# SBUF layout of a fused attention, SoLU and ReLU² kernel: stationary and moving operands of layer 2 on opposite sides

## The chip, the cores and the metric

The kernel runs on one core of a Trainium2 chip. The metric is the device time of one execution in microseconds (us), lower is better. Three runs of the kernel before gave 858.24, 858.86 and 859.9 us, a median of 858.86 us. The profiled execution is a further run, of 858.75 us.

## The reference

```python
scores = q @ k.T / 8 + cum[:, None] - cum[None, :]     # cum = cumsum(log(clip(f))), causal mask
attn   = softmax(scores) @ v                           # 4 batches, 8 heads, 576 tokens, head size 64
x      = attn as [2304 tokens, 512]
h      = x @ w_in                                      # layer 1, w_in [512, 1024]
solu   = h * softmax(h)
x      = layernorm(solu) * g_ln @ w_out                # w_out [1024, 512]
out    = maximum(x @ w2_in, 0) ** 2 @ w2_out           # layer 2, w2_in [512, 2048], w2_out [2048, 512]
```

All of it is float32. The kernel multiplies in fp32r: each operand is split into a high part and the rest, `h` and `l`, and a product is made of three matmuls (high by low, low by high, high by high).

## The kernel before

One program holds attention, layer 1 and layer 2. Each piece of work is added to a planner (`Plan.add`) with its reads, its writes, a priority and a guessed duration for every engine that may do it; `lay` then writes one fixed order for each engine from the guesses. Priorities are planned times: layer 2's weights get `TEND + W20 + p * W2P`, its steps `TEND + P2 + 5200` apart, where `TEND` is the planned end of attention. All DMAs are issued on SyncE's queue in the planned order.

**Layer 2.** The 2,304 tokens are 9 blocks of 256 (`TB`), and the 2,048 hidden features are 8 pairs of 128-wide chunks (`KP`, counted by `p`). `step(blk, p)` has:

- 24 up matmuls (L1175): the stationary operand is a 128x128 piece of the pair's `u` weights (`u0h`, `u0l`, `u1h`, `u1l`), the moving one 256 columns of the block's x tiles (`x2t`, named `vn` in the trace).
- ReLU and square on ScalarE (L1193, L1197), four sums and differences on VectorE (L1204), and the split into `GA`/`GS` by `halves`: the high part by a cast on ScalarE (L341), the rest by a subtraction (L1059) on GpSimd or VectorE, as the planner finds.
- 21 down matmuls (L1229 to L1231): seven products by a Strassen-like scheme, 9 matmuls for group A and 12 for group S; stationary is `GA` or `GS` (named `q` in the trace), moving are 256 columns of the pair's `a`, `b`, `s`, `t` weights.

So a block has 8 x 45 = 360 matmuls of 256 columns and layer 2 has 3,240. TensorE runs the ups of one step, then the downs of the step before it.

`weights2(p)` brings the weights of pair `p` once, between layer 1 and block 0: four loads of 256 KB from `w2d` into raw tiles (`raws`, in turn by `RING`), five splits of 512 and one of 256 columns (`halves`), and four differences of 256 (`diff`, L1096), on GpSimd or VectorE.

**Where tiles lie.** SBUF is handed out in the order of the calls of `new`, so the address of a tile is the sum of the sizes before it. Layer 2 has no room of its own: `carve` reuses the tiles of attention and layer 1 once they are free, and the lists `large` (512 columns), `small` (256) and `upper` (512, taken by the `u` weights of pairs 5 to 7) are filled by `more` and emptied by `place`. In KiB of a partition, counted from the first tile: `maskb` 0, `wih` 1.3, `wil`, `woh`, `wol` to 65, `k1`, `k2` to 109, `qn`, `adj`, `pt`, `x`, `xh`, `xl`, `e`, `free`, `xw` to 157.3, small vectors and `q3`, then `ws` from 159.8, `xc`, `ident` 165.8, `q1` 166.3, `q2` 174.3, `vn` 182.3, `kn` 194.3, `ln` 198.3 to 222.3.

By this the up matmuls have their weights low (`free`, `k1`, `k2`, `pt`, `wih`, `wil`) for pairs 0 to 4 and high (`ln`) for pairs 5 to 7, and their x tiles high (`vn`). The down matmuls have `q1`/`q2` high as stationary and most weights low; the `a` weights of pairs 4 to 7 lie in `ws`, `xc` and `kn`, high.

**Double buffering.** `x2slot` has six x tiles: the first half of a block's features (g = 0) has two sets, the second half one, so that the second half of the next block is loaded after the last ups of this one. At a change of block the ups are done in two lots of 12.

Layer 1's last stage is `out1` (L773 to L775: stationary `woh`/`wol`, moving `ln`). PSUM has three free banks `pp`, of which one is held by `seven` through a block, and two banks `hp` that are layer 1's until block 1.

```python
        for a in "hl":
            W[nm + a] = (small if n == 256 else upper if nm[0] == "u" and p >= KP - 3 else large).pop(0)
            claim(W[nm + a], [("w2", p, nm + a)], prio)
...
    def x2slot(blk, a, g):
        return (0, 1, 4, 5)[2 * (blk % 2) + a] if g == 0 else 2 + a
```

Of the kernel before, what the change touches and what calls it, by code (L numbers as in the profile page):

```python
# [8 lines left out]
F32 = mybir.dt.float32  # L9
F32R = mybir.dt.float32r  # L10
# [3 lines left out]
ALU = mybir.AluOpType  # L14
# [226 lines left out]
def tile_kernel(ctx: ExitStack, tc: tile.TileContext, q, k, v, f, w_in, w_out, g_ln, w2_in, w2_out, out):  # L241
    nc = tc.nc
# [48 lines left out]
    K1 = [new(f"k1{j}", [HH, KW], F32R) for j in range(2)]  # L291
    K2 = [new(f"k2{j}", [HH, KW], F32R) for j in range(2)]
    QN = new("qn", [DM])
    ADJ = [new(f"adj{i}", [AW]) for i in range(NADJ)]
    PT = [new(f"pt{i}", [5 * P]) for i in range(NPT)]
    X = new("x", [NP, P])
# [4 lines left out]
    new("xw", [256])  # L301
    ST = [new(f"st{i}", [2]) for i in range(NST)]
# [3 lines left out]
    new("q3", [512])  # L306
    new("ws", [768])
    new("xc", [768])


    ident = new("ident", [P])
    Q1 = [[new(f"q1{i}{j}", [HH, P], F32R) for j in range(2)] for i in range(2)]
    Q2 = [[new(f"q2{i}{j}", [HH, P], F32R) for j in range(2)] for i in range(2)]
    VN = [new(f"vn{i}", [DM]) for i in range(NV)]
    KN = [new(f"kn{i}", [DM]) for i in range(2)]
# [444 lines left out]
    def out1(blk, ccs, prio, dp):  # L760
# [3 lines left out]
        for cc in ccs:  # L764
            w = slice(cc * P, cc * P + P)
            sk = key()
            for g in range(4):
                def fn(g=g, sk=sk, w=w):
                    px = at(sk)[:, 0 : 2 * P].rearrange("p (r x) -> p r x", x=P)
                    for fc in (2 * g, 2 * g + 1):  # L770
                        hi = LN["h"][:, fc, ring[0] : ring[1] + 1 : step, :]
                        lo = LN["l"][:, fc, ring[0] : ring[1] + 1 : step, :]
                        nc.tensor.matmul(px, lhsT=woh[:, fc, w], rhs=lo, start=(fc == 0), stop=False)  # L773
                        nc.tensor.matmul(px, lhsT=wol[:, fc, w], rhs=hi, start=False, stop=False)  # L774
                        nc.tensor.matmul(px, lhsT=woh[:, fc, w], rhs=hi, start=False, stop=(fc == KF - 1))  # L775

                rk = [(a, r, g // 2) for a in ("lnh", "lnl") for r in ring]
                rk += [("wo", fc, cc // 2, a) for fc in (2 * g, 2 * g + 1) for a in "hl"]
                pl.add(dict(pe=714), fn, prio, rk, [sk], take=sk if g == 0 else None, uses=[sk] if g else [])
                prio += dp / 4  # L780
# [175 lines left out]
    held["maskb"] = ["mask"]  # L956
    held["free"] = [("fr", i, z) for i in range(5) for z in "lh"] + [("fw", i) for i in range(5)]
# [21 lines left out]
    def rk2(ri):  # L979
        return [("2r", ri, z) for z in range(2)]  # L980
# [9 lines left out]
    for j in range(2):  # L990
        more(f"k1{j}", 5, 1)
        more(f"k2{j}", 5, 1)
# [6 lines left out]
    more("xl0", 1)  # L999
    more("e", 2)  # L1000
    for a in ("woh", "wol"):
        more(a, 8)
    for a in ("ln0", "ln1"):
        more(a, 6, 0, upper)
# [3 lines left out]
    for i in range(2):  # L1008
        small.extend(carve(f"kn{i}", [256, 256], old=rk2(i)))
    more("xc", 0, 3)  # L1010
    GS = [carve(f"q1{i}{j}", [512])[0] for i in range(2) for j in range(2)]
    GA = [carve(f"q2{i}{j}", [384])[0] for i in range(2) for j in range(2)]
    x2t = [carve(f"vn{i}", [512])[0] for i in range(4)]
    raws = [carve(a, [512], F32)[0] for a in ("kn0", "kn1", "adj1", "adj2", "vn4", "vn5", "pt4", "x")]

    x2t += [carve(f"vn{i + 4}", [512], old=rk2(i + 4))[0] for i in range(2)]
# [7 lines left out]
    RING = [n % 8 for n in range(4 * (KP - 2))] + [2 + n % 6 for n in range(8)]  # L1024
# [90 lines left out]
    def x2slot(blk, a, g):  # L1115
        return (0, 1, 4, 5)[2 * (blk % 2) + a] if g == 0 else 2 + a
# [38 lines left out]
    def step(blk, p, prio):  # L1155
        g = (blk * KP + p) % 2
        uid[0] += 1
        pool = "hp" if blk and g else "pp"
# [5 lines left out]
        if (blk, p) == (1, 1):  # L1164
            pl.add(dict(dve=0), lambda: None, prio - 5000, [], ["h", "hp"])
        W = W2[p]
        for y, c in ((0, 0), (0, 1), (1, 0), (1, 1)):
# [15 lines left out]
            pl.add(dict(pe=6 * 116), up, prio, rk, [ck], take=None if y + c else ck, uses=[ck] if y + c else [])  # L1183
# [258 lines left out]
W20, W2P, P2 = 30000, 5000, 30000  # L1442
# [53 lines left out]
```

## Time and profile before

| | |
|---|---|
| median of three runs | 858.86 us |
| profiled execution | 858.75 us |
| its span in the trace | 857.0 us |
| around the span | 1.75 us |
| TensorE (PE) busy | 812.9 us, 95% |
| VectorE (DVE) busy | 569.3 us, 66% |
| ScalarE (ACT) busy | 548.7 us, 64% |
| GpSimd (POOL) busy | 396.2 us, 46% |
| DMA | 87.5 MB, 32.7% of 16 engines' span |

PE is matmuls, PEld weight loads, which overlap them; L1175 is line 1175 of the kernel. Matmuls are pipelined: one row of 256 columns shows 0.28 us, but the next one starts 0.11 to 0.12 us later. The distance from start to start is what a matmul costs, and a row that merges n of them lasts n - 1 distances and one 0.28. Times on a timeline are us from the start of the span. A wait is put down to what ended it.

### The profile page before, as it was taken

Reading aid. Unit: us, or ns where it says so; the run is one execution under the profiler, and the core shown is the slowest. Engines: PE = TensorE matmul, PEld = TensorE weight load, DVE = VectorE, ACT = ScalarE, POOL = GpSimd, SP = SyncE. Lnnn points to the kernel's source line nnn. Section 1 sums busy time; section 2 is a strip of 40 time slices with the busy share of each in tenths; the row PEclk is TensorE's granted clock in tenths of the full one; section 3 lists DMA queues with packets and bytes.
Section 4 is the critical chain, followed back from the end, with each engine's and each line's share of the span. In section 5 each row is a group of like instructions: output and inputs, shape, how many; then the busy total and the mean of one; then the engine's idle time right before and its main releaser. Section 6 shows DMA issues by size and latency. Waiting matters only on the chain.

```text
span 857.0 us, 18172 instructions
## 1 busy us (share of the span) xinstructions
PE 812.9 (95%) x6584; PEld 745.0 (87%) x6584; DVE 569.3 (66%) x1371; ACT 548.7 (64%) x1343; POOL 396.2 (46%) x480
## 2 busy tenths in 40 slices
PE   3778999999999999999999989999999999999997
PEld 2556787888888887889899989999999999999996
DVE  7898777878799868855557785454545454554544
ACT  6889989888887878766755644444444444444442
POOL 7547777665676546631397763131312121222221
PEclk9988999999999999999999989999999999999999
DMA  6644336656575565510263330101010101010100
GB/s 206 189 136 134 98 107 196 206 160 195 180 220 161 179 178 164 159 51 26 63 194 114 97 114 26 50 26 50 25 50 26 51 25 50 26 50 26 28 24 25
DMA packets 69338, 87.52 MB, mean 102 GB/s; under 512 B 8480, under 2 KB 46880, under 8 KB 69248
## 3 DMA queue, kind: packets, MB, share of 16 engines
q1 hardware_dynamic: 69248, 86.37, 32.7%
q8 instruction: 51, 0.84, 0.4%
q14 instruction: 39, 0.32, 0.1%
HBM read 63.58 MB, written 22.69 MB: 101 GB/s over the span
## 4 chain that ended last, share of the span: by engine, by line
PE 75%; DVE 10%; ACT 9%; issue 2%; DMA 2%; POOL 1%; SPq 1%; ACTq 0%; DVEq 0%; POOLq 0%
PE pp L1175 12%; PE hp L1175 11%; PE pp L586 5%; PE z L532 4%; PE xo L606 4%; PE z L1230 4%; PE z L1229 4%; PE z L1231 4%; PE hp L832 3%; PE hp L834 3%; PE hp L833 3%; ACT adj L567 3%; PE pp L773 3%; PE pp L774 3%; PE pp L775 3%
## 5 line engine op out<-in xcount | busy, mean ns | idle before, releaser
L1059 POOL TENSOR_TENSOR q<-q,q 128x384 fp32r<-128x384 f32 x72 | 76.6, 1064 | 255.7 <-ACT q L341 209.9
L1204 DVE TENSOR_TENSOR adj<-q 128x256 f32<-128x256 f32 (+1 forms) x144 | 47.8, 374 | 119.8 <-ACT q L1197 119.7
L567 ACT ACTIVATE adj<-z,st 64x288 f32<-64x288 f32 (+9 forms) x192 | 95.3, 499 | 22.7 <-DVE st L553 21.2
L341 ACT CAST q<-adj 128x512 fp32r<-128x512 f32 x70 | 43.4, 620 | 99.4 <-DVE adj L1204 99.4
L532 PE MATMUL z<-k,q 128*128 128x256 f32 (+17 forms) x384 | 94.5, 343 | 10.6 <-DVE q L497 9.0
L586 PE MATMUL pp<-ident,adj 128*128 128x128 f32 (+1 forms) x480 | 78.9, 280 | 18.3 <-ACT adj L567 17.2
L586 PEld LDWEIGHTS pp<-ident,adj 128*128 128x128 f32 (+1 forms) x480 | 51.2, 143 | 45.2 <-ACT adj L567 31.7
L773 PE MATMUL pp<-ln,woh 128*128 128x256 f32 x288 | 82.5, 286 | 0.5 <-DVE ln L912 0.4
L553 DVE CUSTOM_DVE_ANT_0 z<-z,maskb 128x128 f32<-128x128 f32 (+8 forms) x144 | 65.2, 462 | 25.7 <-PE z L532 23.0
L341 ACT COPY pt<-pp 128x256 f32<-128x256 f32 (+5 forms) x169 | 67.2, 420 | 22.4 <-PE pp L586 21.1
L774 PE MATMUL pp<-ln,wol 128*128 128x256 f32 x288 | 80.4, 279 | 0.0
L775 PE MATMUL pp<-ln,woh 128*128 128x256 f32 x288 | 80.2, 278 | 0.0
L532 PEld LDWEIGHTS z<-k,q 128*128 128x128 f32 (+3 forms) x384 | 58.2, 187 | 18.6 <-ACT pt L1334 8.3
L1059 DVE TENSOR_TENSOR q<-adj,q 128x512 fp32r<-128x512 f32 x63 | 44.5, 707 | 42.3 <-ACT q L341 41.5
L1204 DVE TENSOR_TENSOR adj<-adj 128x128 f32<-128x128 f32 x72 | 69.7, 969 | 0.0
L699 POOL TENSOR_TENSOR free<-free 128x256 uint32<-128x256 uint32 x64 | 49.4, 780 | 38.1 <-DVE free L693 25.6
L606 PE MATMUL xo<-pt,vn 128*64 128x128 f32 (+1 forms) x960 | 64.1, 277 | 1.4 <-ACT pt L341 1.3
L606 PEld LDWEIGHTS xo<-pt,vn 128*64 128x64 f32 x960 | 51.4, 142 | 12.3 <-issue 5.6
L832 PE MATMUL hp<-wih,xl 128*128 128x512 f32 x144 | 60.8, 422 | 0.9 <-ACT wih L341 0.9
L833 PE MATMUL hp<-wil,xh 128*128 128x512 f32 x144 | 57.2, 397 | 0.2 <-DVE wil L703 0.2
L834 PE MATMUL hp<-wih,xh 128*128 128x512 f32 x144 | 57.1, 396 | 0.0
L773 PEld LDWEIGHTS pp<-ln,woh 128*128 128x128 f32 x288 | 54.3, 188 | 2.3 <-DVE ln L912 0.9
(386 smaller groups left out, 2498.8 us busy)
## 6 DMA issues: line engine op xcount, KB each, us to landing
x2d<-xc SPq DMA_DIRECT2D x72, 128.0 KB
vn<-x2d SPq DMA_DIRECT2D x36, 256.0 KB
kn<-in_k_dram SPq DMA_DIRECT2D x32, 256.0 KB
free<-in_moe_w_in_dram SPq DMA_DIRECT2D x32, 256.0 KB
free<-in_moe_w_out_dram SPq DMA_DIRECT2D x32, 256.0 KB
w2d<-free SPq DMA_DIRECT2D x64, 128.0 KB
vn<-in_v_dram SPq DMA_DIRECT2D x20, 256.0 KB
out_dram<-adj SPq DMA_DIRECT2D x18, 256.0 KB
```

The costliest lines, as they stand in the source:

```text
L341: nc.scalar.copy(dst(), src())
L532: nc.tensor.matmul(dst, lhsT=ql[0:r, p, 0:m], rhs=rhs, start=(g == 0), stop=(g == 1))
L567: nc.scalar.activation(out=adj[0:m, c[1] : c[2]], in_=Z[c[0]][0:m, 0 : c[2] - c[1]], func=AF.Exp, bias=st[0:m, low : low + 1], scale=-1.0, ...
L586: nc.tensor.transpose(at(sk)[:, (c - g) * m : (c - g + 1) * m], adj[0:m, zc : zc + P], ident[0:m, 0:m])
L606: nc.tensor.matmul(XO[own[j], g // 2, off : off + m], lhsT=VN[vslot[b, c]][:, (g + j) * D : (g + j + 1) * D], rhs=PT[(s - h + g + j) % NPT ...
L773: nc.tensor.matmul(px, lhsT=woh[:, fc, w], rhs=lo, start=(fc == 0), stop=False)
L774: nc.tensor.matmul(px, lhsT=wol[:, fc, w], rhs=hi, start=False, stop=False)
L775: nc.tensor.matmul(px, lhsT=woh[:, fc, w], rhs=hi, start=False, stop=(fc == KF - 1))
L832: nc.tensor.matmul(HP[:, c], lhsT=XL[i][:, cc, :], rhs=wih[:, cc, w], start=(cc == 0), stop=False)
L1059: eng.tensor_tensor(out=lo(), in0=raw(), in1=hi().bitcast(F32), op=ALU.subtract)
L1175: nc.tensor.matmul(ph, lhsT=l[:, w], rhs=r[:, x], start=(y + c + i + k == 0), stop=(y + i == 2 and k == 2), skip_group_check=True,)
L1204: eng.tensor_tensor(out=dst(), in0=x(), in1=y(), op=op)
```

## The change

The order of the calls of `new` is changed, so that in KiB of a partition `k2` comes after `wol` (from 65), then `qn`, `vn` (89.3), `kn`, `pt`, `xh`, `xl`, `e`, `free`, `xw`, `ws`, `xc`, `adj`, `x` and `ident` (to 157.8), small vectors, and then `q1` from 160.8, `q2`, `k1` (176.8) and `ln` (198.8 to 222.8). The `u` weights go to `k1`, `q2` and `ln` for all pairs but 3 and 4, and the last of pair 7 (`u1l`) goes low, since the list is empty by then. The `a` weights' rest of pair 1 lies in `k1`. The x tiles are eight, `vn0` to `vn5`, `kn0` and `kn1`, with two full sets. `kn0`, `kn1`, `vn4` and `vn5`, the second set, are raw tiles of the weights before. Splits and differences of layer 2 are VectorE's alone. Block 0 uses the banks `hp` from pair 1 on. The last `out1` waits for both halves of the normalized tile. Planned times of the weights and steps move by 4 us, and the weights' spacing is 4,500 ns for 5,000.

```diff
-    K1 = [new(f"k1{j}", [HH, KW], F32R) for j in range(2)]
     K2 = [new(f"k2{j}", [HH, KW], F32R) for j in range(2)]
     QN = new("qn", [DM])
-    ADJ = [new(f"adj{i}", [AW]) for i in range(NADJ)]
+    VN = [new(f"vn{i}", [DM]) for i in range(NV)]
+    KN = [new(f"kn{i}", [DM]) for i in range(2)]
...
     new("xw", [256])
+    new("ws", [768])
+    new("xc", [768])
+    ADJ = [new(f"adj{i}", [AW]) for i in reversed(range(NADJ))][::-1]
+    X = new("x", [NP, P])
+    ident = new("ident", [P])
...
-    new("q3", [512])
...
+    new("q3", [640])
...
+    q2 = new("q2", [2, 2, HH, P], F32R)
+    Q2 = [[q2[:, i, j] for j in range(2)] for i in range(2)]
+    K1 = [new(f"k1{j}", [HH, KW], F32R) for j in range(2)]
...
-                rk = [(a, r, g // 2) for a in ("lnh", "lnl") for r in ring]
+                gs = (0, 1) if blk == NTT // 2 - 1 else (g // 2,)
+                rk = [(a, r, y) for a in ("lnh", "lnl") for r in ring for y in gs]
...
+    for j in range(2):
+        more(f"k1{j}", 5, j, upper)
+    c = carve("q2", [512] + [384] * 4)
+    upper.append(c[0])
+    GA = c[1:]
     for a in ("ln0", "ln1"):
         more(a, 6, 0, upper)
...
-    x2t += [carve(f"vn{i + 4}", [512], old=rk2(i + 4))[0] for i in range(2)]
+    x2t += [carve(a, [512], old=rk2(i))[0] for a, i in (("kn0", 0), ("kn1", 1), ("vn4", 4), ("vn5", 5))]
...
-    RING = [n % 8 for n in range(4 * (KP - 2))] + [2 + n % 6 for n in range(8)]
+    RING = [n % 8 for n in range(4 * (KP - 2))] + [0, 1, 2, 3, 4, 5, 0, 1]
...
-            eng = nc.gpsimd if s.on == "pool" else nc.vector
-            eng.tensor_tensor(out=lo(), in0=raw(), in1=hi().bitcast(F32), op=ALU.subtract)
-
-        s = pl.add(dict(pool=119 + 2.213 * n, dve=67 + 1.045 * n), sub, prio, list(rk) + [hk], [lk], port=True)
+            nc.vector.tensor_tensor(out=lo(), in0=raw(), in1=hi().bitcast(F32), op=ALU.subtract)
+
+        pl.add(dict(dve=67 + 1.045 * n), sub, prio, list(rk) + [hk], [lk], port=True)
...
-                W[nm + a] = (small if n == 256 else upper if nm[0] == "u" and p >= KP - 3 else large).pop(0)
+                W[nm + a] = (small if n == 256 else upper if nm[0] == "u" and p not in (3, 4) and upper else large).pop(0)
...
-            s = pl.add(dict(pool=686, dve=335), fn, prio, rk, wk, port=True)
+            pl.add(dict(dve=335), fn, prio, rk, wk, port=True)
...
-        return (0, 1, 4, 5)[2 * (blk % 2) + a] if g == 0 else 2 + a
+        return 4 * (blk % 2) + 2 * g + a
...
-        pool = "hp" if blk and g else "pp"
+        pool = "hp" if (p if blk == 0 else g) else "pp"
...
-        if (blk, p) == (1, 1):
+        if (blk, p) == (0, 1):
...
-            pl.add(dict(pe=6 * 116), up, prio, rk, [ck], take=None if y + c else ck, uses=[ck] if y + c else [])
+            pl.add(dict(pe=6 * 116), up, prio, rk, [ck] + ["turn"] * (y + c == 0), take=None if y + c else ck, uses=[ck] if y + c else [])
...
-W20, W2P, P2 = 30000, 5000, 30000
+W20, W2P, P2 = 34000, 4500, 34000
```

## Rows read from the trace of the kernel before

**Rows 1.** The page: busy time by engine, and the chain that ended last.

```profile
PE 812.9 (95%) x6584; PEld 745.0 (87%) x6584; DVE 569.3 (66%) x1371; ACT 548.7 (64%) x1343; POOL 396.2 (46%) x480
...
PE 75%; DVE 10%; ACT 9%; issue 2%; DMA 2%; POOL 1%; SPq 1%; ACTq 0%; DVEq 0%; POOLq 0%
```

**Rows 2.** Busy time by stretch: from:to, length, each engine (instructions), granted clock, DMA.

```profile
540.00:580.00 40.00, 40.00 (x343) 40.00 (x342) 21.15 (x45) 17.23 (x31) 9.81 (x9) 1.00 0.13 41
```

**Rows 3.** PE's timeline in layer 2: start, length, engine, line, out<-in, form, count.

```profile
607.06 0.28 PE L1229 MATMUL z<-k,q 128*128 128x256 f32 x1
...
609.45 0.87 PE L1175 MATMUL hp<-vn,pt 128*128 128x256 f32 x6
...
612.28 0.28 PE L1229 MATMUL z<-k,q 128*128 128x256 f32 x1
...
614.75 2.90 PE L1175 MATMUL pp<-vn,wil 128*128 128x256 f32 x24
617.48 0.28 PE L1229 MATMUL z<-ws,q 128*128 128x256 f32 x1
...
619.97 3.04 PE L1175 MATMUL hp<-vn,ln 128*128 128x256 f32 x24
...
826.09 2.90 PE L1175 MATMUL pp<-vn,wil 128*128 128x256 f32 x24
```

**Rows 4.** PE's timeline at the end of layer 1.

```profile
458.57 0.28 PE L773 MATMUL pp<-ln,woh 128*128 128x256 f32 x1
...
465.71 0.28 PE L1229 MATMUL xo<-k,q 128*128 128x256 f32 x1
...
467.07 0.28 PE L773 MATMUL pp<-ln,woh 128*128 128x256 f32 x1
...
470.49 0.28 PE L775 MATMUL pp<-ln,woh 128*128 128x256 f32 x1
```

**Rows 5.** PE's timeline in layer 1, first product (xh, xl by wih, wil).

```profile
438.70 0.39 PE L832 MATMUL hp<-wih,xl 128*128 128x512 f32 x1
...
441.87 0.39 PE L834 MATMUL hp<-wih,xh 128*128 128x512 f32 x1
```

**Rows 6.** Groups by form, 540 to 820 us: count | busy us, mean ns | idle before.

```profile
L1059 POOL TENSOR_TENSOR q<-q,q 128x384 fp32r<-128x384 f32 x53 | 56.3, 1063 | 207.5 <-ACT q L341 166.0 <-PE xo L1231 31.7 <-POOL q L1059 5.5
...
L1204 DVE TENSOR_TENSOR adj<-adj 128x128 f32<-128x128 f32 x53 | 52.7, 995 | 0.0
...
L1059 DVE TENSOR_TENSOR q<-adj,q 128x512 fp32r<-128x512 f32 x46 | 31.9, 693 | 31.5 <-ACT q L341 31.5
...
L1204 DVE TENSOR_TENSOR adj<-q 128x256 f32<-128x256 f32 x53 | 22.6, 426 | 99.0 <-ACT q L1197 99.0
...
L1204 DVE TENSOR_TENSOR adj<-adj,q 128x128 f32<-128x128 f32 x53 | 16.4, 310 | 0.0
```

**Rows 7.** Busy time by stretch of 10 us, around PE's gap in block 0.

```profile
490.00:500.00 10.00, 6.83 (x41) 6.23 (x40) 8.79 (x11) 4.94 (x10) 7.93 (x9) 0.80 0.40 100
500.00:510.00 10.00, 10.00 (x74) 9.85 (x73) 8.14 (x14) 6.00 (x11) 6.93 (x8) 0.86 0.43 125
```

**Rows 8.** Groups on POOL and on DVE, 430 to 560 us.

```profile
L1096 POOL TENSOR_TENSOR adj<-adj 128x256 f32<-128x256 f32 x7 | 6.1, 877 | 0.5
...
L1059 POOL TENSOR_TENSOR k<-vn,k 128x512 fp32r<-128x512 f32 x2 | 2.5, 1296 | 0.0
...
L1059 DVE TENSOR_TENSOR ln<-adj,ln 128x512 fp32r<-128x512 f32 x2 | 2.4, 1220 | 0.0
```

**Rows 9.** Timeline of the last step.

```profile
847.07 1.05 POOL L1059 TENSOR_TENSOR q<-q,q 128x384 fp32r<-128x384 f32 x1 [4.31 <-issue]
...
847.17 1.09 DVE L1204 TENSOR_TENSOR adj<-adj 128x128 f32<-128x128 f32 x1
...
848.16 0.39 PE L1229 MATMUL z<-xc,q 128*128 128x256 f32 x1 [0.60 <-POOL q L1059]
...
849.69 0.39 PE L1229 MATMUL xo<-wol,q 128*128 128x256 f32 x1 [0.20 <-DVE q L1059]
```

More of the change, by code (lines that the diff above doesn't have):

```diff
@@ L289, in tile_kernel @@
     woh, wol = (new(t, [KF, DM], F32R) for t in ("woh", "wol"))
-    K1 = [new(f"k1{j}", [HH, KW], F32R) for j in range(2)]
     K2 = [new(f"k2{j}", [HH, KW], F32R) for j in range(2)]
     QN = new("qn", [DM])
-    ADJ = [new(f"adj{i}", [AW]) for i in range(NADJ)]
+    VN = [new(f"vn{i}", [DM]) for i in range(NV)]
+    KN = [new(f"kn{i}", [DM]) for i in range(2)]
     PT = [new(f"pt{i}", [5 * P]) for i in range(NPT)]
-    X = new("x", [NP, P])
     XH = [new(f"xh{i}", [KC, P], F32R) for i in range(XB)]
@@ L305, in tile_kernel @@
     ST1 = [new(f"sm{i}", [16]) for i in range(2)]
-    new("q3", [512])
-    new("ws", [768])
-    new("xc", [768])
-    ident = new("ident", [P])
+    new("q3", [640])
     Q1 = [[new(f"q1{i}{j}", [HH, P], F32R) for j in range(2)] for i in range(2)]
-    Q2 = [[new(f"q2{i}{j}", [HH, P], F32R) for j in range(2)] for i in range(2)]
-    VN = [new(f"vn{i}", [DM]) for i in range(NV)]
-    KN = [new(f"kn{i}", [DM]) for i in range(2)]
+    q2 = new("q2", [2, 2, HH, P], F32R)
+    Q2 = [[q2[:, i, j] for j in range(2)] for i in range(2)]
+    K1 = [new(f"k1{j}", [HH, KW], F32R) for j in range(2)]
     for y in range(2):
@@ L939, in tile_kernel @@
             held[f"q1{i}{j}"] = [("ql", i, j), ("qd", i, j)]
-            held[f"q2{i}{j}"] = [("qh", i, j), ("qa", i, j)]
     held["qn"], held["q3"] = ["qn"], []
@@ L956, in tile_kernel @@
     held["maskb"] = ["mask"]
+    held["q2"] = [(y, i, j) for y in ("qh", "qa") for i in range(2) for j in range(2)]
     held["free"] = [("fr", i, z) for i in range(5) for z in "lh"] + [("fw", i) for i in range(5)]
@@ L990, in tile_kernel @@
     for j in range(2):
-        more(f"k1{j}", 5, 1)
         more(f"k2{j}", 5, 1)
@@ L998, in tile_kernel @@
     more("xh0", 1)
-    more("xl0", 1)
     more("e", 2)
@@ L1007, in tile_kernel @@
     more("maskb", 0, 1)
-    for i in range(2):
-        small.extend(carve(f"kn{i}", [256, 256], old=rk2(i)))
+    more("xl0", 0, 2)
     more("xc", 0, 3)
+    small[-2:-2] = carve("pt4", [256, 256], old=rk2(6))
     GS = [carve(f"q1{i}{j}", [512])[0] for i in range(2) for j in range(2)]
-    GA = [carve(f"q2{i}{j}", [384])[0] for i in range(2) for j in range(2)]
     x2t = [carve(f"vn{i}", [512])[0] for i in range(4)]
     raws = [carve(a, [512], F32)[0] for a in ("kn0", "kn1", "adj1", "adj2", "vn4", "vn5", "pt4", "x")]
-    x2t += [carve(f"vn{i + 4}", [512], old=rk2(i + 4))[0] for i in range(2)]
+    x2t += [carve(a, [512], old=rk2(i))[0] for a, i in (("kn0", 0), ("kn1", 1), ("vn4", 4), ("vn5", 5))]
     OUT = [carve(f"adj{i + 1}", [512], F32, rk2(i + 2))[0] for i in range(2)]
@@ L1094, in fn @@
             def fn():
-                eng = nc.gpsimd if s.on == "pool" else nc.vector
-                eng.tensor_tensor(out=dst(), in0=x(), in1=y(), op=ALU.subtract)
-            s = pl.add(dict(pool=686, dve=335), fn, prio, rk, wk, port=True)
+                nc.vector.tensor_tensor(out=dst(), in0=x(), in1=y(), op=ALU.subtract)
+            pl.add(dict(dve=335), fn, prio, rk, wk, port=True)
         place("a", 256)
```

## The prediction, as it stood before the run

> **What bounds the kernel.** I read the busy times and the chain first. TensorE is busy 95% of the span and makes 75% of the chain that ended last [rows 1]. In layer 2 it has no gap at all: 40.00 of 40 us, at the full granted clock, with VectorE at half load [rows 2]. So what counts there is the distance from one matmul to the next, and the timeline gives it. The ups of pair 4 (wil) start at 614.75 and, five blocks on, at 826.09 [rows 3]: 211.34 / 5 = 42.27 us for a block of 360, 117.4 ns each.
>
> That mean hides three paces. Downs from 607.06 to 609.45: 2.39 us for 21, 113.8 ns. Ups on pt and wih, 609.45 to 612.28, 24: 117.9. Downs to 614.75: 117.6. Ups on wil to 617.48, 24: 113.8. Downs to 619.97: 118.6, the first three of them on ws. Ups on ln: (3.04 - 0.28) / 23 = 120.0 [rows 3]. The form is the same in all, so what differs is where the operands lie. By the sums of the tile sizes, ln, vn, q and ws all lie above 159 KiB of a partition: stationary and moving on the same, upper side cost 120.0. On opposite sides there are two paces, 113.3 and about 117.9, and place alone does not choose: downs (q high, weights low) run at both. The end of layer 1 shows what does change it. Stationary woh/wol low, moving ln high: 63 matmuls from 458.57 to 465.71 take 113.3 ns each. Then come 12 downs with the sides exchanged, at the same pace, 113.3, up to 467.07, and the same L773 to L775 afterwards run at (470.49 - 467.07) / 29 = 117.9 [rows 4]. Among the steps too the pace changes where downs give way to ups [rows 3]. A stretch keeps its pace, then, while the sides stay, and an exchange can turn it.
>
> **The change part by part.**
>
> *Layout.* For pairs 0, 1, 2, 5, 6 and 7 stationary is high and moving low in ups and downs alike, so the exchange at every turn is gone, and so are the 72 ups at 120.0 of pairs 5 to 7. For pairs 3 and 4 both operands of the ups are low. No fp32r row of 256 columns shows that. The nearest low-low stretch, 512 columns of layer 1, takes (441.87 - 438.70) / 14 = 226.4 ns, twice 113.2 [rows 5], so bounds are 113.3 and 120.0. I take 120.0, because there the tiles lie a hundred KiB apart and here, for pair 3, side by side. Four ups of pair 7 (u1l low) and one down of pair 1 (a piece of a in k1, high) I price likewise: 48 + 4 + 1 = 53 at 120.0. The other 307 take 113.3 or 117.9. A block is 53 x 120.0 + 307 x 113.3 = 41.14 us (1.13 less than 42.27) or, with 117.9, 42.56 us (0.29 more). I take 113.3: two exchanges per step are what the rows show moving the pace, and 113.3 is the pace with nothing added. Block 0 waits for its weights anyway (below), so eight blocks count: -9.0, bounds -9.0 and +2.3. With pairs 3 and 4 at 113.3 too the low end falls by 8 x 48 x 6.7 ns = 2.6 more.
>
> The Trainium skill, page "TensorE: Matmul & The Clock Gate", section "Step-by-step: what each phase is for", says that TensorE reads moving and stationary operands through two independent SBUF ports, so that the next weight load takes nothing from the running matmul. By that rule the layout is worth nothing, and the rate term would be 0. The 120.0 beside 113.3 [rows 3, 4] speaks against it, but no row shows the cause.
>
> *Splits on VectorE alone, steady state.* The POOL subtraction of 384 columns (1,063 ns) goes, and VectorE gets one between its 256-wide sum at 426 and its 512-wide split at 693: 560 ns. In return the last 128-wide difference, 995 ns against 310 for its equal, loses the 685 it spends beside the POOL one [rows 6]. VectorE's load per step falls by about 0.1 us, and TensorE covers it: 0. Without that cover each step would gain, not lose.
>
> *Tail.* In the last step POOL's subtraction holds VectorE to 848.26, and group S starts at 849.69 behind a chain of cast and split [rows 9]. Without POOL that chain is 0.69 us earlier, but group A, started at 848.16, needs 9 x 0.117 = 1.05 us first, so S comes about 0.5 us earlier: -0.5 (bounds -0.7 and 0).
>
> *Start of layer 2.* TensorE is busy 6.83 us of 490 to 500, and the granted clock of the two stretches is 0.80 and 0.86 [rows 7]: idle 3.2 us, and (0.20 + 0.14) x 10 = 3.4 us of work lost to the half clock, 6.6 us in all. VectorE is full there. It now takes over nearly all of the 32 differences, some 15 of the weights' splits and eight of the steps', which POOL did: a difference of 877 ns costs about 426, a split of 1,296 about 693 [rows 6, 8], some 26 us in the 90 that POOL was at it (an estimate from these rows). But its own splits, 1,220 ns beside POOL, fall back to 693 [rows 8]: about 27 of them, 14 us, and the steps' differences 8 x 0.69 = 5.5 us more. So 20 of 26 come back, and six are added to a queue in which PE idles. The bank pair hp from pair 1 on relieves the three banks pp, which works the other way. I take 0, with -6.6 (gap gone) and +7 (refund absent) as bounds.
>
> *x tiles.* The same 36 loads of 256 KB are issued on SP's queue. From block 2 on they start a block earlier and nothing waits; the two-lot ups at a change of block cost no gap today [rows 2], so 0. Block 1's set lies in raw tiles that pair 7's last splits must leave first: behind the splits on VectorE stand those loads, and behind them block 1's ups. TensorE has pair 7's ups and two steps' downs, 66 x 0.12 = 8 us, as cover: 0, and up to +4 once if it is gone.
>
> *Layer 1.* The scores' k1 moves up beside q1: 192 of 384 score matmuls become high-high, 192 x 6.7 ns = 1.3 us at most; I take +1.0. For attention's value product (vn and pt now both low) and the transposes (ident low beside adj) I take 0, from the low-low stretch at twice 113.2 [rows 5]; if each of 704 transposes pays 6.7 ns and each of 960 half-width loads 3.3, it is +7.9. The last out1 waits for the second half of its input, one split of some 0.7 us, hidden by the steps already issued: 0. The turn key and the new priorities only order instructions: 0 beyond the start's bounds.
>
> **Sum.** Against the profiled execution, 857.0 + 1.75 = 858.75 (0.11 below the median): 858.75 - 9.0 - 0.5 + 0 + 1.0 = 850.3 us.
>
> **Rivals.**
> 1. *The slow pace holds.* The six pairs settle at 117.9, and with no exchange nothing turns them back. For it: 30 matmuls of constant sides keep it [rows 4], and downs that follow high-high ones run at it [rows 3]. Against: 63 in a row at 113.3 [rows 4]. 858.75 + 2.3 - 0.5 + 1.0 = 861.6, slower. It decides as soon as over three quarters of the 307 run at 117.9.
> 2. *Mixed pace.* The single-sided ups of pairs 3 and 4 turn the pace as an exchange does, and half the matmuls run at each: rate -3.3, 856.0.
> 3. *The layout does nothing to TensorE,* and the paces have another cause: 858.75 - 0.5 = 858.3. This is the change not doing what it says.
>
> **How the numbers follow.** A measurement of this kernel tells about 0.2% (1.7 us) from no change. Forecast 0.50: 850.3, own range 845 to 856 (start at -5, layer 1 at +6). Slow pace 0.22, mixed 0.18, no effect 0.10. Faster: 0.45 + 0.12 + 0.03 = 0.60; same: 0.04 + 0.04 + 0.05 + 0.05 = 0.18 (forecast, slow, mixed, none); slower: 0.01 + 0.18 + 0.01 + 0.02 = 0.22. The range reaches from the forecast's low end to the slow pace with a start 1.4 us late: 845 to 863.
>
> **What would show it.** Right: the ups on ln and k1 leave 120.0 for about 113.3, downs stay there, and a block lasts 41.1 to 41.3 us. Pairs 3 and 4 alone stand out in the timeline. The 128-wide difference falls to about 310 ns, POOL's subtractions are gone from layer 2, and group S starts closer to A in the last step. Wrong: 117.9 in long stretches (rival 1), a change of pace at pairs 3 and 4 (rival 2), 120.0 kept on ln (rival 3), a wider PE gap in block 0 with VectorE full, or matmuls of layer 1 further apart.

## The result, and the profile after

The changed kernel takes 850.91 us in the median of five runs (850.18 to 853.29), against 858.86: a ratio of 0.9911, with a 95% interval of 0.9893 to 0.9929. The forecast was 850.3. The sign and the size came out, and the main mechanism in kind: paces of TensorE that go with the place of its operands. What of the place counts did not come out (it is not the upper and the lower side), and three terms missed by 3.6 to 5.4 us. They have both signs, and that the sum came so close is partly luck (see below).

First the page of the changed kernel, busy time by engine, which answers to [rows 1]. Its profiled execution is the slowest of the five: 853.29 us, span 851.2.

```profile
PE 807.2 (95%) x6584; PEld 740.6 (87%) x6584; DVE 562.2 (66%) x1507; ACT 545.4 (64%) x1337; POOL 258.2 (30%) x350
```

POOL has lost 138 us. TensorE is still the bound, with 5.7 us less of busy time. Next, TensorE's timeline in layer 2 (columns as in [rows 3]): the ups of pairs 3, 4, 5, 6, the first low piece of pair 7's ups, and pair 3 again two blocks later.

```profile
649.36 3.03 PE L1176 MATMUL hp<-vn,pt 128*128 128x256 f32 x24
...
654.61 0.88 PE L1176 MATMUL pp<-vn,wih 128*128 128x256 f32 x6
...
659.87 2.88 PE L1176 MATMUL hp<-vn,ln 128*128 128x256 f32 x24
...
665.06 2.99 PE L1176 MATMUL pp<-vn,ln 128*128 128x256 f32 x24
...
671.18 0.28 PE L1176 MATMUL hp<-vn,wol 128*128 128x256 f32 x1
...
732.55 3.03 PE L1176 MATMUL hp<-vn,pt 128*128 128x256 f32 x24
```

How to read them: a row of 24 lasts 23 distances and one matmul of 0.28 us. So 3.03 or 3.04 is a pace of 120 ns, 2.99 is 117.8, and 2.88 is 113. The ups on ln stood at 3.04 in all three pairs before ([rows 3] show the first). Now pair 5 runs at 113 and pair 6 at 117.8: the pace is mixed, as rival 2 had it. But the 24 slow ups of pair 4 are followed by the fast pace; it turned between pairs 5 and 6, which have the same places by region. A block lasts (732.55 - 649.36) / 2 = 41.60 us against 42.27.

The start of layer 2, busy time by stretch, answers to [rows 7]:

```profile
470.00:480.00 10.00, 8.58 (x70) 8.18 (x70) 5.90 (x13) 5.02 (x13) 1.11 (x1) 1.00 0.61 194
480.00:490.00 10.00, 9.72 (x84) 9.52 (x83) 7.77 (x22) 6.98 (x14) 0.51 (x1) 1.00 0.29 80
490.00:500.00 10.00, 10.00 (x87) 10.00 (x87) 9.83 (x24) 6.67 (x13) 0.00 (x0) 1.00 0.22 57
500.00:510.00 10.00, 7.99 (x60) 7.59 (x59) 7.35 (x18) 3.73 (x7) 0.53 (x1) 0.89 0.60 181
510.00:520.00 10.00, 10.00 (x82) 10.00 (x82) 5.87 (x17) 3.91 (x7) 0.00 (x0) 0.94 0.15 55
```

The gap that stood at 490 is gone, and one of 2.0 us stands at 500, with a granted clock of 0.89 and 0.94 behind it. Idle time and slow clock together are 2.0 + 1.1 + 0.6 = 3.7 us, against 6.6 before. Another 1.7 us of idle time stand from 470 to 490, where the kernel before had none: 5.4 in all. The timeline at 504 says what the gap there is (start, length, engine, idle time before and its releaser):

```profile
504.30 1.36 SPq L1128 DMA_DIRECT2D kn<-x2d  x2
...
504.59 0.69 DVE L1061 TENSOR_TENSOR wol<-kn,wol 128x512 fp32r<-128x512 f32 x1 [0.32 <-ACT wol L342]
...
506.34 0.38 PE L1230 MATMUL z<-xc,q 128*128 128x256 f32 x1 [1.55 <-DVE q L1061]
...
510.85 1.76 PE L1176 MATMUL pp<-kn,k 128*128 128x256 f32 x12
```

The two loads of block 1's x tiles into kn are issued only from 504.30 on, when the last splits of pair 7 are leaving it. Block 1's ups start at 510.85, so TensorE has nothing to put between pair 7's ups and its downs, and waits 1.55 us for the step's split on VectorE.

### The profile page after: what moved, and what is told of

Read it like the earlier page. It is cut to its first block, busy times and chain, and to the rows that moved or that the text cites. A ratio compares the mean times of both kernels' runs of the same rounds, so it can differ in the third digit from the quotient of the medians.

```text
span 851.2 us, 18065 instructions
## 1 busy us (share of the span) xinstructions
PE 807.2 (95%) x6584; PEld 740.6 (87%) x6584; DVE 562.2 (66%) x1507; ACT 545.4 (64%) x1337; POOL 258.2 (30%) x350
## 4 chain that ended last, share of the span: by engine, by line
PE 77%; ACT 9%; DVE 8%; issue 3%; DMA 1%; POOL 1%; SPq 0%; ACTq 0%; DVEq 0%; POOLq 0%
PE hp L1176 13%; PE pp L1176 11%; PE pp L587 5%; PE z L533 5%; PE xo L607 4%; PE z L1232 4%; PE z L1231 4%; PE z L1230 4%; PE pp L774 3%; PE pp L775 3%; PE pp L776 3%; PE hp L834 3%; ACT adj L568 3%; PE hp L836 3%; PE hp L835 3%
## 5 line engine op out<-in xcount | busy, mean ns | idle before, releaser
L1205 DVE TENSOR_TENSOR adj<-q 128x256 f32<-128x256 f32 (+1 forms) x144 | 45.1, 354 | 132.4 <-ACT q L1198 132.4
L342 ACT COPY pt<-pp 128x384 f32<-128x384 f32 (+5 forms) x168 | 66.8, 420 | 23.0 <-PE pp L587 21.6
L1061 DVE TENSOR_TENSOR q<-adj,q 128x512 fp32r<-128x512 f32 x72 | 49.7, 690 | 41.6 <-ACT q L342 41.6
L607 PE MATMUL xo<-pt,vn 128*64 128x128 f32 (+1 forms) x960 | 61.9, 272 | 1.4 <-ACT pt L342 1.4
L1194 ACT ACTIVATE hp<-hp 128x512 f32<-128x512 f32 x39 | 22.7, 582 | 62.8 <-PE hp L1176 62.8
L1194 ACT ACTIVATE pp<-pp 128x512 f32<-128x512 f32 x33 | 19.2, 582 | 61.7 <-PE pp L1176 61.7
```

The lines of the kernel that those rows point to most:

```text
L342: nc.scalar.copy(dst(), src())
L607: nc.tensor.matmul(XO[own[j], g // 2, off : off + m], lhsT=VN[vslot[b, c]][:, (g + j) * D : (g + j + 1) * D], rhs=PT[(s - h + g + j) % NPT ...
```

## The experiments

All on TensorE's side turn on one question: is it the upper and the lower region that count, as predicted, or something in the addresses that goes with them? By the sizes in the order of `new`, every tile that a matmul reads starts at a multiple of 128 bytes, counted from the first tile, or at 64 more; the first tile lies at byte 1152 (run 1's expectation), itself a multiple of 128. In the kernel before, of the operands of matmuls, at remainder 0 lie q1, q2, vn, kn, ln, ws, xc and the transposes' ident, all high, and **maskb, which is low**. In the changed kernel q1, q2, k1 and ln lie there, and again maskb; everything else is at 64. Pieces of a tile keep its remainder. So two theories fit the 256-column matmuls of both kernels, and maskb, which carries a down piece of pair 4 in the changed kernel, is where they part.

**1. maskb moved by 64 bytes** (the changed kernel):

```diff
-    maskb = new("maskb", [S + 64], BF16)
     gcol = new("gcol", [KF])
     mhalf = new("mhalf", [1])
+    maskb = new("maskb", [S + 64], BF16)
```

> The changed kernel with one allocation moved: maskb (which holds one down piece of pair 4 in layer 2) goes behind gcol and mhalf, from byte 1152 of a partition (a multiple of 128) to byte 1216 (64 more than one). Theory A (half-lines): a matmul pays when the stationary tile loaded for the next one and the moving tile of the running one start at the same remainder, 0 or 64, of 128 bytes, and single payers turn the pace. Then pair 4's downs no longer turn at 120.0+ into 117.8; the 90 matmuls from there to pair 7's ups run at 113.3 instead of 117.8, -0.40 us in each of blocks 1 to 8, so about 847.7 us; if wol in pair 7 then turns the pace the other way, the stretch behind it pays 0.4 to 0.6 a block and the time is 850 to 852. Theory B (regions, as predicted): maskb lies low in both kernels, nothing changes, pair 4's downs still turn to 117.8, 850.9 us.

852.79 us, ratio 0.9932 (0.9914 to 0.9951). The ups of pair 6, those of pair 7 about its first wol piece, and block 5's first ups:

```profile
663.47 2.88 PE L1176 MATMUL pp<-vn,ln 128*128 128x256 f32 x24
668.57 0.96 PE L1176 MATMUL hp<-vn,ln 128*128 128x256 f32 x7
669.37 0.28 PE L1176 MATMUL hp<-vn,wol 128*128 128x256 f32 x1
...
673.86 1.57 PE L1176 MATMUL pp<-kn,k 128*128 128x256 f32 x12
```

The same 12 ups in the changed kernel:

```profile
675.57 1.52 PE L1176 MATMUL pp<-kn,k 128*128 128x256 f32 x12
```

Pair 6 has gone from 2.99 to 2.88, which theory B doesn't allow: maskb was and is low. But wol's pieces (64 beside 64) now turn fast into slow, where in the changed kernel they turned slow into fast: 12 ups on k take 1.57 us instead of 1.52. This is theory A's second branch. A block lasts 41.90 us instead of 41.60. A few matmuls out of line turn the pace, and in either direction.

**2 to 4. Shifts by 64 and by 128 bytes**: unused bytes in front of a tile, which move it and what follows within its region. In 2 and 3 q3 also gives up 128 floats to make room, so q1, q2, k1 and ln move down by 384 bytes, which leaves their remainder by 128 and changes that by 256.

```diff
 (2: the changed kernel)
+    new("gap0", [16])
     VN = [new(f"vn{i}", [DM]) for i in range(NV)]
     KN = [new(f"kn{i}", [DM]) for i in range(2)]
+    new("gap1", [16])
 (3: the changed kernel)
+    new("gap0", [32])
     VN = [new(f"vn{i}", [DM]) for i in range(NV)]
 (4: the kernel before)
+    new("gap0", [16])
     for y in range(2):
         new(f"ln{y}", [KF * 3 * P])
```

> The changed kernel with 64 bytes of nothing ahead of vn and 64 behind kn, so that the x tiles of layer 2 (vn, kn), the moving operands of all ups, go from remainder 64 to remainder 0 of 128 bytes and stay in the lower region; every other tile keeps its remainder. Theory A (half-lines): the 144 ups per block of pairs 0 to 2 and 5 to 7 go to 120.0, the 48 of pairs 3 and 4 leave 120.0 for 113.3 or 117.8; net 96 x about 5 ns = +0.5 us a block, 853 to 857 us. Theory B (regions): no pace changes, 850.9 us.

> Control for the shift: the changed kernel with 128 bytes of nothing ahead of vn, so that tiles move but none changes its remainder of 128 bytes nor its region. Theories A and B both: every pace as in the changed kernel (120.0 in the ups of pairs 3 and 4 alone), 850.9 us within 1. A theory by which 64 bytes matter through the sheer shift of later tiles gives a changed pace here as well.

> The kernel before with 64 bytes of nothing ahead of ln0: ln goes from remainder 0 to 64 of 128 bytes and stays in the upper region. Theory A (half-lines): the 72 ups per block on ln (pairs 5 to 7) leave 120.0 for 113.3 or 117.8, -0.16 to -0.48 us a block, and in layer 1 the last product (woh/wol stationary, ln moving, both now at 64) goes from 113.3 to 120.0, at most 1 us in all; 855 to 858 us. Theory B (regions): the ups on ln stay at 120.0 and layer 1 at 113.3; 858.9 us.

The fourth is the cleanest: 856.50 us, ratio 0.9974 (0.9961 to 0.9987). Its timeline has two rows of layer 1's last product that lie 50 matmuls apart, and the ups on ln:

```profile
460.67 0.28 PE L775 MATMUL pp<-ln,wol 128*128 128x256 f32 x1
...
466.67 0.28 PE L774 MATMUL pp<-ln,woh 128*128 128x256 f32 x1
...
667.24 2.90 PE L1176 MATMUL pp<-vn,ln 128*128 128x256 f32 x24
```

In layer 2, ln beside vn has gone from 120.0 [rows 3] to (2.90 - 0.28) / 23 = 113.9, though both still lie high. In layer 1 the 50 distances take 6.00 us, 120.0 each, where ln beside woh and wol took 113.3 [rows 4], though they lie over 130 KiB apart. One shift of 64 bytes does both, in opposite directions. **For matmuls of 256 columns the region plays no part; the remainder by 128 decides whether one costs about 120.0.** The rule does not reach the 512-column ones of [rows 5]: there stationary (xl, xh) and moving tiles (wih, wil) all lie at 64, and a matmul takes 226.4 ns, twice 113.2. Why is not shown.

The second says the same from the other side: 859.80 us. Its ups on k1 and ln, high beside low but now 0 beside 0, run at 120.0, and those on pt leave it:

```profile
642.30 3.04 PE L1178 MATMUL hp<-vn,k 128*128 128x256 f32 x24
...
652.99 2.99 PE L1178 MATMUL hp<-vn,pt 128*128 128x256 f32 x24
...
663.58 3.04 PE L1178 MATMUL hp<-vn,ln 128*128 128x256 f32 x24
```

It lost 8.9 us where 2 to 6 were expected, because nearly all the rest ran at 117.8; a block lasts 42.55 us. The third, meant as a control, missed altogether: 858.55 us in place of 850.9. Its pair 3 is at 120.0 as expected (3.03), but the ups on ln, and most else, run at 117.8, 42.38 us a block:

```profile
649.71 3.03 PE L1177 MATMUL hp<-vn,pt 128*128 128x256 f32 x24
...
660.36 2.99 PE L1177 MATMUL hp<-vn,ln 128*128 128x256 f32 x24
```

So the remainder by 128 says who pays, and not which of the other two paces holds. On that the next runs bear. Pair 4's ups show a limit of the rule itself: here wih and wil lie at 192 by 256 and vn at 64, equal by 128 alone, and their 24 distances, from 655.04 to 657.89, scatter between 115 and 122 with a mean of 118.8. Every steady 120.0 of this study is of tiles that are equal by 256 too.

**5 to 7. The exceptions taken away**, three in 5, pair 4's ups also in 6, pair 3's also in 7 (5 and 7 shown; 6 has 7's wih and not its pt). The tile k11 gets 64 floats more, in 6 and 7 wih too, and q3 gives up 128:

```diff
 (5: the changed kernel, with maskb as in 1)
-    for j in range(2):
-        more(f"k1{j}", 5, j, upper)
+    more("k10", 5, 0, upper)
+    c = carve("k11", [512] * 5 + [16, 256])
+    upper.extend(c[:5])
+    small.append(c[6])
-    small[-2:-2] = carve("pt4", [256, 256], old=rk2(6))
+    upper.append(carve("pt4", [48, 512], old=rk2(6))[1])
+    last = large.pop()
+    small[-2:-2] = [(lambda: last[0]()[:, 0:256], last[1]), (lambda: last[0]()[:, 256:512], last[1])]
 (7: on top of 5)
+    u3 = [carve(f"pt{i}", [48, 512])[1] for i in range(4)]
+    c = carve("wih", [48] + [512] * 4 + [16] + [512] * 4)
+    u4 = c[1:5]
+    large.extend(c[6:])
+    more("wil", 8)
...
+    upper[12:12] = u3 + u4
```

> The changed kernel with the three single exceptions to the 64-byte rule gone: maskb behind gcol and mhalf (to remainder 64), pair 1's low piece of a 64 bytes further on in k11 (to 64), and the low half of pair 7's second up weight in pt4 at an offset of 48 floats (from 64 to 0) instead of in wol, pair 6's a going to wol. All tiles keep their regions. Only the ups of pairs 3 and 4 still have both operands at 64. Theory A (64-byte remainder): nothing turns the pace, 48 ups at 120.0 and 312 matmuls at 113.3, 41.12 us a block against 41.60, about 847 us. Theory B (regions): k11's piece is still high beside high, the piece in pt4 low beside low, maskb low; the pace turns as before, 850.9 us. A third way: the pace turns without any exception; then 117.8 shows up in places where both theories have none.

> As the one before, and the four up weights of pair 4 lie in wih shifted by 48 floats, so at remainder 0 while still low; only pair 3's 24 ups have both operands at 64. Theory A: pair 4's ups go from 120.0 to 113.3 though both operands are low; 336 at 113.3 and 24 at 120.0, 40.96 us a block, about 845.7 us. Theory B: pair 4's ups stay at 120.0, 850.9 us.

> As the one before, with pair 3's up weights in pt0 to pt3 shifted by 48 floats as well: all stationary operands of layer 2 at remainder 0, all moving ones at 64, no exception left in a block. Theory A: no 120.0 anywhere and one pace from the first block to the last: 113.3 gives 40.80 us a block and about 844.4 us; if it is caught in the slow one, 117.8, 42.40 us a block and about 857 us, since nothing turns it any more. Theory B: pairs 3 and 4, low beside low, stay at 120.0; 850.9 us.

In turn 846.36 us (ratio 0.9858, 0.9841 to 0.9874), 846.93 (0.9865, 0.9852 to 0.9879) and 856.28 (0.9975, 0.9963 to 0.9987). Pair 3's ups in two blocks of each, two blocks apart, and an up group of pair 6, 4 and 6 in turn; of 7 also a wait in block 0:

```profile
644.69 3.04 PE L1181 MATMUL hp<-vn,pt 128*128 128x256 f32 x24
...
660.31 2.88 PE L1181 MATMUL pp<-vn,ln 128*128 128x256 f32 x24
...
726.93 3.04 PE L1181 MATMUL hp<-vn,pt 128*128 128x256 f32 x24
```

```profile
645.27 3.04 PE L1185 MATMUL hp<-vn,pt 128*128 128x256 f32 x24
650.53 2.88 PE L1185 MATMUL pp<-vn,wih 128*128 128x256 f32 x24
...
727.19 3.04 PE L1185 MATMUL hp<-vn,pt 128*128 128x256 f32 x24
```

```profile
473.38 0.28 PE L1184 MATMUL hp<-vn,q 128*128 128x256 f32 x1
...
474.06 0.84 PE L1184 MATMUL hp<-vn,pt 128*128 128x256 f32 x6
475.57 1.68 PE L1184 MATMUL hp<-vn,pt 128*128 128x256 f32 x12 [0.67 <-ACT hp L1202]
...
647.71 2.99 PE L1184 MATMUL hp<-vn,pt 128*128 128x256 f32 x24
...
663.61 2.99 PE L1184 MATMUL pp<-vn,ln 128*128 128x256 f32 x24
...
732.51 2.99 PE L1184 MATMUL hp<-vn,pt 128*128 128x256 f32 x24
```

Blocks of 41.12, 40.96 and 42.40 us, each the expected figure to the last digit. The whole gain that the forecast took for the layout (41.14 a block) is thus there to be had, once the three single exceptions are out. Pair 4's ups in 6 run at the fast pace though both their tiles lie low: once more the remainder, not the region. And the version without any exception is the worst of the three: its one pace, 117.8, holds through all blocks. It was not so from the outset. Up to the wait at 475.57 the pace was 113.3 (six distances in 0.68 us from 473.38 to 474.06); behind it, with no tile at another remainder, it is 117.8, and stays. A wait can turn the pace, then, though not every one does: in the changed kernel the gap at 504.5 has 113.3 ahead of it and 117.8 behind it. In 5 and 6 the 24 or 48 ups at 120.0 cost 6.7 ns each and, from block 1 on, are followed by the fast pace every time, so they also mend what the waits of block 0 did. Between 5 and 6 the medians show no difference: 6's blocks are 0.16 us shorter, but its block 1 ended 0.9 us later.

**8. 128 bytes in front of vn again, now in version 5.**

```diff
+    new("gap0", [32])
     VN = [new(f"vn{i}", [DM]) for i in range(NV)]
```

> The version at 846.4 us (exceptions only in the ups of pairs 3 and 4) with 128 bytes of nothing ahead of vn. Remainders by 128 stay as they are, so no new exception arises; by 256 the moving tiles below vn (k2, wih to wol) stay at 192 and those above (vn, kn, free, xw, ws, xc) go to 64. Theory A1 (only the remainder by 128 counts): every pace as without the gap, 113.3 but for 48 ups at 120.0, 846 us. Theory A2 (the pace turns also where the moving operand passes from one remainder by 256 to the other): 117.8 comes back in the downs and ups behind such passages, 41.5 to 42.4 us a block, 849 to 857 us, as the first 128-byte gap cost the changed kernel 7.6 us.

856.94 us, ratio 0.9977 (0.9966 to 0.9987), with blocks of 42.33 us, so not A1. The downs behind pair 3's ups show the turn:

```profile
651.60 0.28 PE L1236 MATMUL z<-xw,q 128*128 128x256 f32 x1
...
651.94 0.28 PE L1236 MATMUL z<-k,q 128*128 128x256 f32 x1
652.06 0.28 PE L1237 MATMUL z<-qn,q 128*128 128x256 f32 x1
...
653.94 0.28 PE L1238 MATMUL xo<-k,q 128*128 128x256 f32 x1
```

On xw and ws (64 by 256) three distances take 0.34 us, 113. Where the moving operand passes to k2 and qn (192 by 256) the pace turns: 16 distances from 652.06 to 653.94, 117.5 each. Without the gap, with all at 192, the same downs stay at 113 (version 5: six distances from 647.91 to 648.59 in 0.68 us). Run 3 turns at the same place: three distances from 652.58 to 652.92 in 0.34 us, then 17 up to 654.92 in 2.00. Whether the moving tile's own remainder does it, as A2 has it, or its distance from the stationary tile, is not settled: the turn is the same by either.

**9 and 10. The part that isn't layout**: splits and differences on VectorE alone, done alone on the kernel before, and undone alone in the changed one. The edit, forwards and backwards, is the one of the change's diff at these lines:

```diff
-            eng = nc.gpsimd if s.on == "pool" else nc.vector
-            eng.tensor_tensor(out=lo(), in0=raw(), in1=hi().bitcast(F32), op=ALU.subtract)
+            nc.vector.tensor_tensor(out=lo(), in0=raw(), in1=hi().bitcast(F32), op=ALU.subtract)
...
-            s = pl.add(dict(pool=686, dve=335), fn, prio, rk, wk, port=True)
+            pl.add(dict(dve=335), fn, prio, rk, wk, port=True)
```

> The kernel before with one part of the change alone: the splits' subtractions and the weights' differences run on VectorE only. By the prediction's sum TensorE covers it in the steady blocks (0), the start of layer 2 comes out even (0, bounds -6.6 and +7) and the tail gains at most 0.5: 858.4 us within 1, paces unchanged. Rival: freeing the subtractions from POOL is a part of the gain; then 855 or less, with the gap in block 0 shorter.

> The changed kernel with one part undone: the splits' subtractions and the weights' differences may go to POOL again. Theory: that part alone was worth 5.9 us on the kernel before, nearly all in the first two blocks; undone here it costs the same, 855 to 858 us, the blocks from 2 on keep 41.6 us each, and TensorE's gap in block 0 is longer. Rival: its worth hangs on the layout and order of before; then it costs under 2 us here.

Alone it takes 852.74 us, ratio 0.9934 (0.9919 to 0.9948): 5.9 us, on the rival's side and not the expected 0. Undone it gives 862.23, ratio 1.0037 (1.0023 to 1.0051): 11.3 us more than the changed kernel (10.8 by the ratios), and slower than before. That is neither the 5.9 expected nor the rival's 2; blocks from 2 on keep their 41.60 us, as expected. The stretches about the start of layer 2, of the kernel before (up to [rows 7]), of the one and of the other:

```profile
470.00:480.00 10.00, 10.00 (x89) 9.98 (x88) 6.30 (x11) 6.92 (x16) 7.28 (x7) 1.00 0.51 157
480.00:490.00 10.00, 10.00 (x88) 10.00 (x87) 7.92 (x13) 5.56 (x11) 6.23 (x7) 1.00 0.18 54
```

```profile
470.00:480.00 10.00, 8.48 (x72) 8.09 (x71) 9.44 (x25) 7.93 (x19) 0.62 (x1) 1.00 0.59 184
480.00:490.00 10.00, 10.00 (x87) 10.00 (x87) 8.96 (x23) 6.89 (x13) 0.85 (x1) 1.00 0.33 88
490.00:500.00 10.00, 10.00 (x86) 10.00 (x86) 8.62 (x22) 5.30 (x10) 0.85 (x1) 1.00 0.16 47
```

```profile
490.00:500.00 10.00, 7.31 (x55) 6.50 (x54) 7.99 (x10) 4.99 (x10) 7.54 (x8) 0.98 0.11 26
500.00:510.00 10.00, 8.99 (x62) 8.59 (x62) 7.79 (x10) 5.12 (x10) 7.66 (x9) 0.85 0.51 140
510.00:520.00 10.00, 5.93 (x33) 5.53 (x34) 5.28 (x7) 2.48 (x5) 5.64 (x6) 0.83 0.33 99
```

With the subtractions on VectorE the gap of [rows 7] is gone; 1.5 us of idle time stand at 470 to 480, and the granted clock stays at 1.00. VectorE does 25, 23 and 22 instructions in the three stretches from 470 to 500 where it did 11, 13 and 11. Block 1 ends at 550.86 instead of 556.29 (0.5 of the 5.4 us was there when attention ended), and the blocks behind it are as long as before (42.29). With POOL in the changed kernel TensorE is idle for 7.8 us in these 30, and the clock falls to 0.83; TensorE's longest wait there is on POOL's split of q, 3.0 us.

**11 and 12. The order of the raw tiles**, in the changed kernel and in version 6:

```diff
-    RING = [n % 8 for n in range(4 * (KP - 2))] + [0, 1, 2, 3, 4, 5, 0, 1]
+    RING = [n % 8 for n in range(4 * (KP - 2))] + [2, 3, 0, 1, 4, 5, 2, 3]
```

> The changed kernel with another order of the raw tiles for the weights of pairs 6 and 7: 2, 3, 0, 1, 4, 5, 2, 3 in place of 0, 1, 2, 3, 4, 5, 0, 1, so that kn0 and kn1 (raw 0 and 1), which hold block 1's first x tiles, are free one pair earlier. Theory: the gap that TensorE has at 504.5 us in the changed kernel, with the lower granted clock behind it (2.0 us idle and about 1.7 of slow work), is block 1's first ups waiting for x tiles that load into kn0 and kn1 only when pair 7's last splits have left them; then the gap goes, the clock stays at 1.00, and the time falls by 3 to 4 us to about 847.3. Rival: the gap is pair 7's own chain of splits on a full VectorE; then it stays and the time is 850.9.

> The version with pair 3's ups as the only exception to the 64-byte rule (40.96 us a block) and the other order of raw tiles together. If the two gains are independent: about 3.5 us below either 846.4 or 846.9, so 843 to 844 us, blocks of 40.96 us from block 1 on. Rival: the gap in block 0 merely moves to another wait; then 846.5.

The first takes 848.66 us, ratio 0.9874 (0.9859 to 0.9889). Its timeline and stretch:

```profile
499.31 0.36 SPq L1128 DMA_DIRECT2D kn<-x2d  x1
...
504.93 1.52 PE L1176 MATMUL pp<-kn,k 128*128 128x256 f32 x12
...
507.65 0.28 PE L1230 MATMUL z<-xc,q 128*128 128x256 f32 x1
```

```profile
500.00:510.00 10.00, 10.00 (x90) 10.00 (x89) 8.12 (x22) 5.62 (x11) 0.00 (x0) 1.00 0.55 170
```

The loads into kn are issued at 497.04 and 499.31 instead of 504.3 and 505.3, block 1's ups stand ahead of pair 7's downs, the gap is gone and the clock stays at 1.00. Block 1 ends at 551.52 instead of 555.75, 4.2 us earlier; the medians give 2.3 and the ratios, each against its own runs of before, (0.9911 - 0.9874) x 858.9 = 3.2. The second, 844.80 us, ratio 0.9821 (0.9804 to 0.9837), is the fastest version of this study. It beats version 6 by 2.1 in the medians and 3.8 by the ratios; its block 1 ended 1.1 us before version 6's, in a run whose attention ended 0.3 later.

## Why the prediction was right, and where it wasn't

- **Paces (-9.0 predicted; -5.4 measured, 8 x (42.27 - 41.60)).** The mechanism was right as to kind: by the place of its operands a matmul costs 120.0, or 113.3 or about 117.9, and an exchange can turn the pace. The step that failed is "on opposite sides ... I take 113.3: two exchanges per step are what the rows show moving the pace". A few matmuls out of line turn it too: the piece of a in k1, maskb, and u1l in wol, of which two had been priced at 6.7 ns apiece and maskb not seen at all. The block came out 41.60 - 41.14 = 0.46 us longer, which at 4.5 ns is about 100 of the 307 at 117.8. Rival 2 has its share in this: "the single-sided ups of pairs 3 and 4 turn the pace", but to the fast one, which is what follows them. With these exceptions away the blocks came to 41.12 (run 5). The same step priced the fast pace as the one that holds by itself; run 7, with no exchange at all, ran at the slow one.
- **"Side" as region.** The sides of the prediction were the halves of SBUF. Run 4 shows that they are the two remainders by 128 bytes; the allocation of both kernels had let the two go together but for maskb. So the forecast was right on a mechanism that was not the one at work: on these two kernels both give nearly the same list of pairs.
- **Low beside low** at 120.0 for pairs 3 and 4: right (3.03 for 24), by one of two bounds and for the wrong reason, "side by side". wih lies over 80 KiB from kn and pays as much. The other bound, 113.3, came from 512-column matmuls that lie at equal remainders and do not pay, so these rows could not stand for the ups.
- **Start of layer 2 (0 predicted, -5.4 measured in run 9).** The step "20 of 26 come back, and six are added to a queue in which PE idles" weighed engine times over the whole start and left out when they fall. The six came out: from 440 to 530 us VectorE is busy 64.6 us before and 70.3 in run 9. But they went where VectorE had room: it is busy 35.0 of the 50 us from 440 to 490 before and 46.1 in run 9, and from 490 to 530 29.7 and 24.2. "VectorE is full there" holds for the gap's stretches alone. Before, only 0.7 of the gap's 3.2 us ended with POOL's split; 1.5 ended with a cast on ScalarE and 1.0 with a split on VectorE, which took 1.34 us beside POOL for 0.69 alone. The bound of -6.6, "gap gone", was the nearer one. The refund that was bounded came in full, as the groups of the changed kernel, 540 to 820 us, show (a 128-wide difference at 285 against 995 [rows 6], the 512-wide split at 691 as before):

```profile
L1061 DVE TENSOR_TENSOR q<-adj,q 128x512 fp32r<-128x512 f32 x54 | 37.3, 691 | 32.3 <-ACT q L342 32.3
...
L1205 DVE TENSOR_TENSOR adj<-adj 128x128 f32<-128x128 f32 x54 | 15.4, 285 | 0.0
```

  The Trainium skill, page "SBUF — State Buffer", section "Who interferes with whom", says that a VectorE operation with two inputs in SBUF contends with a GpSimd instruction that reads SBUF. The trace agrees: 995 ns beside POOL's subtraction, 285 without it.

- **x tiles (0 predicted, "up to +4 once if it is gone"; +4.2 in the profiles of run 11, 3.2 by the ratios).** The chain was named correctly: splits, loads, block 1's ups. The cover was not there, because the two steps' downs that were to give it belong to pairs 6 and 7, and pair 7's own wait for the step's split on VectorE.
- **Steady VectorE load (0), tail (-0.5).** The first is right: runs 9 and 10 change no block after the first two. Of the tail, the last block became shorter by 0.93 us where the others lost 0.67, so about -0.25. Group S did not move closer to A (843.97 behind 842.19, 1.78 us against 1.53 [rows 9]): A's own wait shrank, from 0.88 us behind the matmul before it to 0.34.
- **Layer 1 (+1.0 predicted).** The last out1 began 1.8 us later, of which 0.55 was there when attention ended. That was not taken apart; across the fourteen kernels attention ended between 427.3 and 431.4 us, so half a microsecond is within what its runs vary.

The terms as measured for layer 2, -5.4 - 0.25 - 5.4 + 4.2, make -6.9 where the sum had -9.5; the last matmul moved from 851.09 to 845.33, by 5.8, so 1.1 us were lost ahead of layer 2, where the sum had 1.0. Of the 3.6 us by which the rate fell short, start and x tiles together gave back 1.2. The rest, 2.7 us, and 0.3 around the span (2.1 against 1.75) are the 3.0 by which the profiled execution lies above the forecast; it lies 2.4 above the median of its runs. So the median comes within 0.6 us of the forecast by luck as well: by terms that missed in both directions, and by the spread of the runs. By the ratio the change is worth (1 - 0.9911) x 858.9 = 7.6 us, 0.9 less than forecast. The start's -5.4 is of run 9, on the old layout; the banks, the new priorities and the wait of the last out1 were not run alone. Rival 3 (the layout does nothing) and rival 1 (the slow pace holds) are out for this kernel, but rival 1's way is what run 7 took: one pace, 117.8, and nothing behind block 0 that turned it back.

The parts do not add: splits on VectorE alone are worth 5.9 us with the old order and 11.3 with the new, and the rest of the change without them makes the kernel 3.4 us slower.

## What to carry to other kernels

Where matmuls follow each other without a gap, read the distance between their starts by operand and keep the tiles that serve as stationary and those that serve as moving operands at different remainders of 128 bytes. That alone is not enough: run 7 does it everywhere and is 10 us slower than version 5, which leaves 48 ups out of line. So look at which of the two remaining paces holds, and at what turned it: small leftovers, and waits of TensorE. When a resource is double-buffered into space that another stage still uses, find the last user of each piece and give it the pieces that are wanted last: here eight numbers in a list were worth 3 us. A change of several parts needs each part run alone; this one had a gain and a loss of 4 to 5 us each that the total didn't show.

## What was not expected of the hardware

- At a granted clock of 1.00 the distance of 128x256 fp32r matmuls takes three steady values, 113.3, 117.8 and 120.0 ns, or 272, 282.7 and 288 periods of 2.4 GHz for 256 columns. Stationary and moving tile at the same remainder of 128 bytes: 120.0 (87 of the last 94 distances in layer 1 of run 4), steady only where they are equal by 256 as well (run 3). At different ones: 113.3 or 117.8, and it stays. It is a matmul's own two tiles that count by these rows, not the next one's stationary tile: in run 5 the last down before pair 3's ups, moving at 64 ahead of a stationary tile at 64, takes 113 ns, and the last up, ahead of one at 0, takes 121. With 512 columns nothing of it shows [rows 5]. The Trainium skill, page "SBUF — State Buffer", section "Who interferes with whom", has TensorE's two reads of SBUF on independent ports and TensorE waiting for no one. Here 64 bytes in an address are worth 6.7 ns per matmul, so where page and runs differ, the runs decide; why they do is not shown.
- The pace among the two is a state. It held from block 0's waits to the last block in run 7, and turned at few exceptions (the changed kernel, run 1), where the moving tile's remainder by 256 changed (run 8), and at waits (run 7, the changed kernel). What sets it, and why 24 ups at 120.0 are followed by the fast one in versions 5 and 6, stays open.
- In the changed kernel TensorE's 2.0 us of idle time at 504 to 508 cost nearly as much again, 1.7 us, in granted clock: 0.89 and 0.94 in the two stretches, of which a part is at 1.2 GHz. Run 11, without that gap, has 1.00 there, and the 1.5 us idle of run 9 at 470 to 480 cost none (1.00).
